# PSUM banks dealt out anew in a gated S4D and Infini-attention kernel: maxima, spreading products, and the last segment's skip

## The chip, the cores and the metric

The kernel runs on one core of one Trainium2 chip. The metric is the device time of one execution in microseconds, lower is better. Before the change three runs took 926.03, 926.98 and 929.62 us; the median is 926.98.

## What is computed

The input is one sequence `x` of 2048 rows and 448 channels. Two branches are computed from it and mixed by a gate `g = sigmoid((x * gate_w).sum(-1))`:

```
a   = fftconv(x, K) + x * D_skip        # K: an S4D kernel of 2048 taps for each channel
q, k, v = x @ wq, x @ wk, x @ wv        # 16 heads of 28, 4 segments of 512 rows
for each segment s:
    a_dot = softmax(q k^T / sqrt(28) + causal mask) v
    a_mem = phi(q) M / (phi(q) z + 1e-6)       # M, z: sums over earlier segments
    o     = sigmoid(beta) a_mem + (1 - sigmoid(beta)) a_dot
    M, z  = M + phi(k)^T v, z + sum phi(k)     # phi(t) = t + 1 if t > 0 else exp(t)
b   = o @ wo
out = g * a + (1 - g) * b
```

For the first segment `M` and `z` are zero.

## The kernel before, in words

**Two halves.** The first half (`first_half`, to about 497 us) makes the S4D kernel's taps and projects q, k and v. The change does not touch it. The second half (`second_half`) does the attention and the convolution, and everything below belongs to it.

**PSUM in the second half.** PSUM has eight banks of 128 x 512 floats. `psum_pool` deals them out by tags, and `k.ps(tag)` takes the next buffer of a tag by turns: "m" one bank, "a" three buffers of two banks, "pv" one bank. TensorE's instructions stay in program order (`k.mm`, `k.tr`). A product into a buffer waits until whoever reads the buffer's last contents has finished. The order of VectorE, ScalarE, GpSimd and SP is laid by a planner that simulates the timeline, except for what is pinned (`k.pin`) or put behind a mark (`k.dma`, `k.ldma`).

**Attention in groups.** There are 16 groups, i = 4 * segment + head group, of four heads (of 32 partitions each). A group passes through three generators.

- `maxima(i)` finds the row maxima of the scores in six steps, each for one pair of heads and one of three pieces of the causal triangle: piece 0 is 512 columns, piece 1 is 384 and 128, piece 2 is 256. A step takes one "a" buffer, a head to each bank. VectorE adds the mask and takes the maximum in one operation (L927, followed by a short read of the accumulator into `mx`). After six steps four transposes (L1270) bring `mx` into "m", ScalarE (L937) and VectorE (L938) negate it into `mn`, and a DMA issued by GpSimd (L939) writes it into the q tile, so that the weights' product subtracts the maximum by itself.
- `weigh(i)` computes the scores again, transposed, in six steps with an "a" buffer each. ScalarE takes the exponential into `PT` (L958), and GpSimd masks the diagonal (L969).
- `values(i)` multiplies `PT` by V into "pv", and ScalarE copies that into `pvs` (L989).

**The loop.** In round i there are six steps; each issues one step of maxima(i + 2), one of weigh(i), and in groups 1 to 12 on average 1.15 steps of the convolution (`RATIO`). In the second step the values of group i - 1 and the last step of maxima(i + 1) come in between. Before the loop, `transform_k` runs eight blocks with two "a" buffers each, and maxima(0) is interleaved with it; then come maxima(1), with the transposes of maxima(0) behind its third step, and in round 0 maxima(2) beside weigh(0).

**The convolution** (`convolve`) is a product in the frequency domain: for each of 32 chunks `transform` (TensorE into "a", ScalarE copy L569 to `ks`), `product` (TensorE into "a", VectorE multiply L574 to `pr`), and for every second one `back` (eight products into "a", ScalarE copy L587, store). In rounds 14 and 15 `finish` does the last transform in eight calls of `last`: eight products into "a", two VectorE operations (L638) that add the gated result to a tile `rest`, and stores. `join` loads `rest` from TB, `load_b` loads the products' input `bt`.

**Between segments** (`seg_end`): `norm` divides the values by the softmax sums. The sums go through DMAs (`dn`, `RD`, `r8`), and one product per head group (L1267, `ps_m<-r,sel`) spreads the four reciprocals over 32 partitions each. VectorE multiplies (L1046) and adds the memory part (L1048). `recall` does the same for the memory of the next segment (VectorE L1024). Between them four products with `wo` (po) are copied by ScalarE (L1062); `skip` loads a tile of x, multiplies it by `D_skip` (`k.dbc`) on GpSimd (L1056), and `store` adds it, gated, on VectorE (L1063). All these products, and the transposes of the maxima, share the one bank "m". The last segment is treated differently: `skip_last` (called in round 11) writes only the gated skip to TB, `norm(3, 0, 3)` normalises three head groups in round 15, and `last_end` does the fourth through a product with `den` and adds the attention part last.

In `skip_last` GpSimd multiplies by `D_skip` (L1056) and VectorE then by the gate (L1071, a tensor_scalar).

Of the kernel before, what the change touches and what calls it, by code (L numbers as in the profile page):

```python
# [12 lines left out]
F32 = mybir.dt.float32  # L13
# [4 lines left out]
ALU = mybir.AluOpType  # L18
# [5 lines left out]
D = 448  # L24
# [3 lines left out]
SEG = 512  # L28
# [843 lines left out]
def attend(nc, k, ap):  # L872

    v = nc.vector
# [30 lines left out]
    PLACES = ([(0, 0, 512)], [(1, 0, 384), (3, 384, 128)], [(2, 0, 256)])  # L905

    def maxima(i):


        q, kk = Q[i], K[i]  # L910
        mx = ap.tile([128, 4, 4], F32, tag="mx", name="mx", bufs=2)
        for b, hp in MSTEPS:
            pt = k.ps("a")
            for t, o, n in PLACES[b]:
                qt = 3 - t
                for x in range(2):
                    h = 2 * hp + x
                    r = slice(32 * h, 32 * h + 32)
                    k.mm(
                        pt[:, x, o : o + n], q[r, 0, 128 * qt : 128 * qt + 128], kk[r, 0, :n],  # L920
                        start=True, stop=True, tile_position=(32 * h, 0),
                    )
            for t, o, n in PLACES[b]:
                for x in range(2):
                    h = 2 * hp + x
                    junk = ap.tile([128, SEG], F32, tag="jk", name="jk", bufs=1)
                    v.tensor_tensor_reduce(  # L927
                        junk[:, :n], pt[:, x, o : o + n], k.mk[:, SEG - n :], 1.0, -3e38,
                        ALU.add, ALU.max, mx[:, 3 - t, h : h + 1],
                    )  # L930
            yield
        yield
        pm = k.ps("m")
        for qt in range(4):
            k.tr(pm[:4, 128 * qt : 128 * qt + 128], mx[:, qt], k.ident)
        mn = ap.tile([4, 2, SEG], F32R, tag="mn", name="mn", bufs=2)
        nc.scalar.activation(mn[:, 0], pm[:4], AF.Copy, scale=-1.0)  # L937
        v.scalar_tensor_tensor(mn[:, 1], pm[:4], -1.0, mn[:, 0], ALU.mult, ALU.subtract)  # L938
        k.pdma(q.rearrange("(j e) i q -> e j i q", e=32)[28].bitcast(F32), mn.bitcast(F32))  # L939
        yield  # L940
# [51 lines left out]
    def inverse(x, rows, h0, h1, dst, queue):  # L992


        f = 16 * (h1 - h0)
        rc = ap.tile([128, 64], F32, tag="rc", name="rc", bufs=1)
        rs = ap.tile([128, 2, 64], F32R, tag="rs", name="rs", bufs=1)
        v.reciprocal(rc[:, :f], x)
        v.tensor_copy(rs[:, 0, :f], rc[:, :f])
        v.tensor_tensor(rs[:, 1, :f], rc[:, :f], rs[:, 0, :f], ALU.subtract)  # L1000
        rd = k.dr.tile([2, 4, 32 * f], F32, tag=f"RD{f}", name="RD", bufs=2)
        queue(rd.rearrange("b j (i f) -> (j i) b f", f=f), rs[:, :, :f].bitcast(F32))
        queue(
            dst[rows : rows + 8, h0:h1].rearrange("p h q -> p (h q)").bitcast(F32),
            rd.rearrange("b j q -> (b j) q"),
        )
# [3 lines left out]
    def recall(s):  # L1010

        am[s] = ap.tile([128, 4, SEG], F32, tag="am", name="am", bufs=1)
        k.ldma(am[s], k.AM[:, :, s - 1].rearrange("h p q -> p h q"))
        dn = ap.tile([128, 64], F32, tag="dm", name="dm", bufs=1)
        k.ldma(dn, k.DM[s - 1].rearrange("j h (i f) -> (j h i) f", f=64))
        k.pin(v.tensor_scalar(dn, dn, 1e-6, None, ALU.add))
        r8[s] = ap.tile([40, 4, SEG], F32R, tag="r8", name="r8", bufs=1)
        inverse(dn, 32, 0, 4, r8[s], k.pdma)
        for _ in range(3):
            yield  # L1020
        for hg in range(4):
            pb = k.ps("m")
            k.mm(pb, k.sel[32:40], r8[s][32:40, hg], start=True, stop=True)
            v.scalar_tensor_tensor(am[s][:, hg], am[s][:, hg], k.gh[:, hg : hg + 1], pb, ALU.mult, ALU.mult)  # L1024
            yield

    def norm(s, h0, h1, queue):

        pvs = pvss[s]
        f = 16 * (h1 - h0)  # L1030
        dn = ap.tile([128, 64], F32, tag="dn", name="dn", bufs=1)
        for j in range(4):
            queue(
                dn[32 * j : 32 * j + 32, :f],
                pvs[32 * j + 28 : 32 * j + 29, h0:h1].rearrange("o h q -> o (h q)").rearrange("o (i f) -> o i f", f=f),
            )
        if s == 0:
            r8[s] = ap.tile([40, 4, SEG], F32R, tag="r8", name="r8", bufs=1)
        inverse(dn[:, :f], 0, h0, h1, r8[s], queue)
        for _ in range(4):  # L1040
            yield
        for hg in range(h0, h1):
            o = pvs[:, hg]
            pb = k.ps("m")
            k.mm(pb, k.sel[0:8], r8[s][0:8, hg], start=True, stop=True)
            v.scalar_tensor_tensor(o, o, k.omg[:, hg : hg + 1], pb, ALU.mult, ALU.mult)  # L1046
            if s > 0:
                v.tensor_tensor(o, o, am[s][:, hg], ALU.add)  # L1048
            yield

    def skip(s, t):

        i = 4 * s + t
        xt = ap.tile([128, D], F32, tag="xt", name="xt", bufs=4)
        k.ldma(xt, k.u[128 * i : 128 * i + 128])
        k.pin(nc.gpsimd.tensor_tensor(xt, xt, k.dbc, ALU.mult))  # L1056
        return xt
# [8 lines left out]
    def skip_last():  # L1066

        for t in range(4):
            xt = skip(3, t)
            i = 12 + t  # L1070
            v.tensor_scalar(xt, xt, k.gt[:, i : i + 1], None, ALU.mult)  # L1071
            k.dma(k.TB[128 * i : 128 * i + 128], xt)

    def out_mm(s, t, po, hgs):
# [6 lines left out]
    def seg_end(s):  # L1081
        yield from norm(s, 0, 4, k.pdma)
        memory = recall(s + 1)
        for t in range(4):
            xt = skip(s, t)
            po = k.ps("m")
            out_mm(s, t, po[:, :D], range(4))
            store(s, t, po[:, :D], xt)
            next(memory)
            yield  # L1090
        yield from memory
# [27 lines left out]

    k.load_wo = load_wo  # L1120
    k.load, k.maxima, k.weigh, k.values, k.seg_end = load, maxima, weigh, values, seg_end
    k.norm, k.last_end, k.skip_last = norm, last_end, skip_last


# [104 lines left out]
def gated_mix(ctx, tc, k):  # L1229
# [72 lines left out]
    def pool(stack, name, side="left"):  # L1302
        return stack.enter_context(tc.tile_pool(name=name, bufs=1, side=side, reuse_waits="tile"))
# [71 lines left out]
    def psum_pool(stack, shapes):  # L1375
        p = stack.enter_context(tc.tile_pool(name="ps", bufs=1, space=PSUM, reuse_waits="tile"))

        def ps(tag):
            shape, bufs = shapes[tag]
            return p.tile(shape, F32, tag=tag, name="ps_" + tag, bufs=bufs)  # L1380

        k.ps = ps
# [44 lines left out]
    with ExitStack() as st:  # L1427
        psum_pool(
            st,
            {"m": ([128, 512], 1), "a": ([128, 2, 512], 3), "pv": ([128, 512], 1)},  # L1430
        )
        ap = pool(st, "ap", "right")
        k.mk = ap.tile([128, 512], F32, name="mk")
        nc.sync.dma_start(k.mk, k.c_mk)
        k.dbc = ap.tile([128, D], F32, name="dbc")
        tp, cs = ExitStack(), ExitStack()

        def fourier():
            tp.close()
            kst.close()  # L1440
            return pool(cs, "fp")

        def final():
            cs.close()
            return pool(st, "fin")

        second_half(nc, k, ap, pool(tp, "tp"), fourier, final)
# [34 lines left out]
```

## Time and profile before

| what | value |
|---|---|
| median of three runs | 926.98 us (926.03 to 929.62) |
| the profiled execution's own time | 931.7 us |
| its span, first to last instruction | 930.0 us |
| mean granted TensorE clock | 0.879 |
| TensorE products, busy | 756.6 us (81%) |
| TensorE weight loads, busy | 410.9 us (44%) |
| VectorE busy | 578.8 us (62%) |
| ScalarE busy | 549.4 us (59%) |
| GpSimd busy | 180.3 us (19%) |
| HBM | 90.92 MB read, 60.68 MB written |

The profile is that of one execution. In its rows PE is TensorE's products, PEld its weight loads, DVE VectorE, ACT ScalarE, POOL GpSimd, and SPq the queue of the engine that issues most DMAs. A row of the timeline gives the start in us from the beginning of the span, the duration of what is merged in it, engine, line, operation, output<-inputs, and the count; in brackets stands the time for which the engine was idle before, and who ended it. A row of a tile or a line gives the shortest, median and longest duration in ns, and the first and last start. A row of the waits gives who waited for whom: the total in us, how often, and the longest. Most products stand under L1267, since one helper issues them; the tile names tell them apart: `ps_a<-ku,qu` are the maxima, `ps_a<-qu,ku` the weights, `ps_a<-gk,cf`, `ps_a<-gu,cf` and `ps_a<-pr,cb` the convolution's three products, `ps_a<-bt,fc` the last transform, `ps_a<-kb,s1k` the first one. The granted clock is 1.0 at full speed.

### The profile page before, as it was taken

The numbers are of one execution on the slowest core, as the hardware profiler recorded it, in microseconds if no ns is written. First come the engines' busy times: TensorE is split into PE (matmuls) and PEld (weight loads), VectorE is DVE, ScalarE is ACT, GpSimd is POOL, SyncE is SP. The second block draws the span as 40 slices with busy tenths as digits, with TensorE's granted clock in tenths as the row PEclk, the third lists the DMA queues.
The fourth block names the chain that finished last, engine by engine and source line by source line (L and its number), as shares of the span: only waits on it lengthen the run. The fifth ranks groups of instructions, "written<-read, shape, count | busy, mean of one in ns | idle before, by whom it ended". The sixth has DMA issues, their size and how long they took to land.

```text
span 930.0 us, 18810 instructions
## 1 busy us (share of the span) xinstructions
PE 756.6 (81%) x7426; PEld 410.9 (44%) x7426; DVE 578.8 (62%) x1122; ACT 549.4 (59%) x659; POOL 180.3 (19%) x228
## 2 busy tenths in 40 slices
PE   2428968998889987899877699889987998978957
PEld 1314635655456544465533254444443443334423
DVE  8981776477665876657754856655574757565333
ACT  4645798788897898978892244544454444332300
POOL 3821001110011011110010021222312223223210
PEclk9858998999789999899987858988999998688968
DMA  8664622353233433234445984574565654564971
GB/s 212 205 207 142 204 79 71 110 166 126 79 129 101 155 116 113 89 100 160 160 140 200 372 261 148 181 236 157 176 209 189 196 198 157 185 219 127 267 210 39
DMA packets 85786, 153.21 MB, mean 165 GB/s; under 512 B 20034, under 2 KB 53818, under 8 KB 85650
## 3 DMA queue, kind: packets, MB, share of 16 engines
q1 hardware_dynamic: 78434, 140.88, 47.3%
q10 hardware_dynamic: 5792, 9.86, 3.0%
q0 software_dynamic: 1472, 1.27, 0.5%
q8 instruction: 58, 0.95, 0.4%
q14 instruction: 30, 0.25, 0.1%
HBM read 90.92 MB, written 60.68 MB: 163 GB/s over the span
## 4 chain that ended last, share of the span: by engine, by line
PE 49%; DVE 13%; ACT 13%; DMA 12%; issue 6%; SPq 4%; POOL 2%; ACTq 0%; DVEq 0%; POOLq 0%
PE ps_m L1267 19%; PE ps_a L1267 15%; PE ps_arg L1267 5%; PE ps_k L1267 4%; ACT cs L1239 4%; PE ps_pv L1267 3%; DVE jk L927 3%; DVE Y L385 2%; PE ps_m L1270 2%; ACT L1239 2%; SPq L322 2%; DMA dn<-pvs 1%; DVE X L381 1%; DMA qu<-mn 1%; DVE pr L574 1%
## 5 line engine op out<-in xcount | busy, mean ns | idle before, releaser
L927 DVE CUSTOM_DVE_ANT_0 jk<-ps_a,mk 128x512 f32<-128x512 f32 (+3 forms) x256 | 124.9, 488 | 45.2 <-PE ps_a L1267 38.3
L958 ACT ACTIVATE PT<-ps_a 128x1024 f32<-128x1024 f32 (+1 forms) x96 | 84.3, 881 | 112.6 <-PE ps_a L1267 107.7
L347 POOL TENSOR_TENSOR EX<-EX,cab 128x1024 f32<-128x1024 f32 x28 | 53.6, 1913 | 367.8 <-ACT EX L1239 367.8
L1239 ACT ACTIVATE cs<-ps_arg 128x1024 f32<-128x1024 f32 x112 | 108.1, 1019 | 7.1 <-PE ps_arg L1267 5.9
L1267 PE MATMUL ps_a<-qu,ku 32*128 32x512 f32 (+3 forms) x768 | 97.3, 380 | 5.4 <-DMA qu<-mn 2.8
L1267 PE MATMUL ps_m<-xh,w 112*128 112x512 f32 x256 | 95.1, 423 | 4.5 <-DMA w<-WD 3.0
L1267 PE MATMUL ps_k<-Y,X 128*32 128x64 f32 x3584 | 68.7, 235 | 25.3 <-DVE Y L386 25.3
L381 DVE TENSOR_TENSOR X<-EX,cs 128x1024 f32<-128x1024 f32 x56 | 68.4, 1221 | 25.3 <-ACT cs L1239 23.0
L1267 PEld LDWEIGHTS ps_k<-Y,X 128*32 128x32 f32 x3584 | 59.1, 119 | 54.3 <-DVE Y L386 40.0
L969 POOL TENSOR_SCALAR_AFFINE_SELECT PT<-PT 128x256 f32<-128x256 f32 (+1 forms) x96 | 47.5, 497 | 177.2 <-ACT PT L958 166.9
L1267 PEld LDWEIGHTS ps_a<-qu,ku 32*128 32x128 f32 x768 | 67.6, 211 | 18.0 <-DVE mx L927 6.7
L387 DVE SCALAR_TENSOR_TENSOR Y<-EY,cs 128x512 f32<-128x512 f32 x56 | 38.5, 687 | 48.1 <-ACT cs L1239 39.9
L385 DVE TENSOR_TENSOR Y<-EY,cs 128x1024 f32<-128x1024 f32 x56 | 68.3, 1219 | 0.0
L1239 ACT ACTIVATE cs<-cs,bhp 128x1024 f32<-128x1024 f32 x56 | 64.4, 1150 | 1.8
L1267 PE MATMUL ps_a<-ku,qu 32*128 32x512 f32 (+3 forms) x256 | 50.5, 425 | 17.8 <-DVE mx L927 16.6
L1267 PEld LDWEIGHTS ps_m<-xh,w 112*128 112x128 f32 x256 | 49.4, 193 | 30.2 <-issue 15.1
L1239 ACT ACTIVATE EY<-ps_arg 128x1024 f32<-128x1024 f32 x55 | 56.2, 1040 | 6.8 <-PE ps_arg L1267 6.7
L1267 PEld LDWEIGHTS ps_a<-ku,qu 32*128 32x128 f32 x256 | 24.2, 203 | 78.5 <-DVE mx L927 41.7
L1267 PE MATMUL ps_m<-xl,w 112*128 112x512 f32 x128 | 51.4, 401 | 0.0
L1267 PE MATMUL ps_arg<-ct,lh 64*128 64x512 bf16 x224 | 43.3, 400 | 8.8 <-ACT cs L1239 8.3
L574 DVE TENSOR_TENSOR pr<-ps_a,ks 128x896 f32<-128x896 f32 x32 | 34.8, 1086 | 20.7 <-PE ps_a L1267 19.8
L1267 PEld LDWEIGHTS <-lh 64*128 64x128 bf16 x392 | 21.8, 97 | 57.7 <-issue 41.9
(193 smaller groups left out, 1375.5 us busy)
## 6 DMA issues: line engine op xcount, KB each, us to landing
w<-WD SPq DMA_DIRECT2D x32, 448.0 KB
qu<-QD SPq DMA_DIRECT2D x16, 512.0 KB
ku<-KD SPq DMA_DIRECT2D x16, 512.0 KB
GU<-gs SPq DMA_DIRECT2D x32, 224.0 KB
GK<-gs SPq DMA_DIRECT2D x8, 896.0 KB
gk<-GK SPq DMA_DIRECT2D x32, 224.0 KB
gu<-GU SPq DMA_DIRECT2D x32, 224.0 KB
BB<-bs ACTq DMA_DIRECT2D x16, 448.0 KB
```

Of the source, the lines that this page charges most:

```text
L322: nc.sync.dma_start(lt[J][r, c], k.SD[0:2, :, pc, :, n].rearrange("f s q j n -> (f s) (q j) n"))
L347: nc.gpsimd.tensor_tensor(o, o, cab, ALU.mult)
L381: v.tensor_tensor(X, ex, t[:, :, 0], ALU.mult)
L385: v.tensor_tensor(Y[:, :, :, :32], lo, y[:, :, :, ::-1], ALU.mult)
L387: v.scalar_tensor_tensor(Y[:, 1, :, 32:], ey[:, :, 32:], -1.0, y[:, 1], ALU.mult, ALU.mult)
L574: nc.vector.tensor_tensor(pr[c], pt, ks.pop(c), ALU.mult)
L927: v.tensor_tensor_reduce(junk[:, :n], pt[:, x, o : o + n], k.mk[:, SEG - n :], 1.0, -3e38, ALU.add, ALU.max, mx[:, 3 - t, h : h + 1],)
L958: nc.scalar.activation(PT[:, 2 * hp : 2 * hp + 2, 512 * b : 512 * b + n], pt[:, :, :n], AF.Exp, scale=SCALE)
L969: nc.gpsimd.affine_select(sl, sl, pat, ALU.is_ge, 0.0, base=0, channel_multiplier=-1)
L1239: x = op(*args, **kw)
L1267: tc.keep_in_program_order(nc.tensor.matmul(*args, **kw))
L1270: tc.keep_in_program_order(nc.tensor.transpose(*args))
```

## The change

The eight banks are dealt out anew: "a" has two buffers of two banks, not three, and the two banks go to a new tag "x" with two buffers of one bank. A step of maxima takes two "x" tiles, one for each of its two heads, where it took one "a" tile. VectorE reduces one head's pieces first and then the other's, where it alternated between heads; the products' order stays. `recall` puts its spreading products into "pv" in place of "m"; `norm` uses "pv" for even head groups and "m" for odd ones. In `skip_last` the GpSimd product and the tensor_scalar become one VectorE operation with two tensor inputs and the gate as a scalar; loads and stores are the same.

```diff
@@ maxima @@
-            pt = k.ps("a")
+            pt = [k.ps("x") for _ in range(2)]
             for t, o, n in PLACES[b]:
                 qt = 3 - t
                 for x in range(2):
                     h = 2 * hp + x
                     r = slice(32 * h, 32 * h + 32)
                     k.mm(
-                        pt[:, x, o : o + n], q[r, 0, 128 * qt : 128 * qt + 128], kk[r, 0, :n],
+                        pt[x][:, o : o + n], q[r, 0, 128 * qt : 128 * qt + 128], kk[r, 0, :n],
                         start=True, stop=True, tile_position=(32 * h, 0),
                     )
-            for t, o, n in PLACES[b]:
-                for x in range(2):
+            for x in range(2):
+                for t, o, n in PLACES[b]:
                     h = 2 * hp + x
                     junk = ap.tile([128, SEG], F32, tag="jk", name="jk", bufs=1)
                     v.tensor_tensor_reduce(
-                        junk[:, :n], pt[:, x, o : o + n], k.mk[:, SEG - n :], 1.0, -3e38,
+                        junk[:, :n], pt[x][:, o : o + n], k.mk[:, SEG - n :], 1.0, -3e38,
                         ALU.add, ALU.max, mx[:, 3 - t, h : h + 1],
                     )
@@ recall @@
-            pb = k.ps("m")
+            pb = k.ps("pv")
@@ norm @@
-            pb = k.ps("m")
+            pb = k.ps(("pv", "m")[hg % 2])
@@ skip_last @@
-            xt = skip(3, t)
             i = 12 + t
-            v.tensor_scalar(xt, xt, k.gt[:, i : i + 1], None, ALU.mult)
+            xt = ap.tile([128, D], F32, tag="xt", name="xt", bufs=4)
+            k.ldma(xt, k.u[128 * i : 128 * i + 128])
+            v.scalar_tensor_tensor(xt, xt, k.gt[:, i : i + 1], k.dbc, ALU.mult, ALU.mult)
             k.dma(k.TB[128 * i : 128 * i + 128], xt)
@@ gated_mix, second half @@
-            {"m": ([128, 512], 1), "a": ([128, 2, 512], 3), "pv": ([128, 512], 1)},
+            {"m": ([128, 512], 1), "a": ([128, 2, 512], 2), "x": ([128, 512], 2), "pv": ([128, 512], 1)},
```

## The prediction, written before the result was known

> **What bounds the kernel now.** The page's first line gives the span; then I read the windows view, the waits, the timeline.
>
> ```profile
> span 930.0 us, 18810 instructions
> ```
>
> All edits lie behind 497 us, where the first product over ps_a starts. Two stretches of the windows view (at the end of a row stand the granted clock, the DMA engines' busy share and GB/s):
>
> ```profile
> 497.00:546.00 49.00, 38.55 (x235) 20.26 (x235) 33.76 (x108) 15.49 (x18) 3.82 (x8) 0.74 0.96 327
> 546.00:862.00 316.00, 277.86 (x1838) 127.31 (x1842) 185.35 (x530) 135.21 (x166) 79.34 (x134) 0.88 0.56 185
> ```
>
> In the long middle TensorE is busy 277.9 of 316.0 us, VectorE 185.4, ScalarE 135.2: TensorE sets the pace, and only its 38 idle us and its clock (0.88) can give anything. The waits of TensorE from 540 to 860 us say who ends that idle time:
>
> ```profile
> PE ps_a L1267 <- DVE mx L927: 13.4, 18, 3.4
> PE ps_a L1267 <- DVE pr L574: 10.2, 15, 4.4
> PE ps_m L1267 <- ACT tb L1062: 3.6, 5, 0.7
> PE ps_m L1267 <- DVE am L1024: 2.9, 4, 1.0
> ```
>
> The columns are us in total, times, the longest. The first row is the maxima; the 4.4 in the second is the last segment's skip, as shown below; the last two are users of the single bank "m" that wait for each other.
>
> **Part 1, the maxima's own banks: +3.2 and -0.5 us.** In the steady loop (groups 1 to 12) a step allocates one tile for maxima, one for weights, one or two for the convolution. With three buffers by turns, and three tiles a step, each kind reuses its own last tile. With two of "a" for weights and convolution and "x" for maxima that stays so. So no distance in the loop changes, but for the steps with two convolution products, where the second now waits for the weights' exponentials of its step; held against the starts of the trace, one place is short:
>
> ```profile
> 777.41 1.02 ACT L958 ACTIVATE PT<-ps_a 128x1024 f32<-128x1024 f32 x1 [0.50 <-PE ps_m L1267]
> ```
>
> ```profile
> 778.14 1.02 PE L1267 MATMUL ps_a<-gu,cf 64*128 64x448 f32 x4
> ```
>
> The buffer comes free at 778.43, the product began at 778.14: **+0.3**.
>
> What does the split of heads buy? TensorE runs in order, and a step's second head still waits for the last reduction of the step before: the first may start sooner, but the weights behind the second may not. VectorE saves the 0.48 us for which it waits on TensorE after such a stall:
>
> ```profile
> 562.30 0.42 DVE L927 CUSTOM_DVE_ANT_0 jk<-ps_a,mk 128x256 f32<-128x256 f32 x1 [0.48 <-PE ps_a L1267]
> ...
> 563.56 1.09 DVE L574 TENSOR_TENSOR pr<-ps_a,ks 128x896 f32<-128x896 f32 x1 [0.35 <-ACT PT L958]
> ```
>
> Here the next product idles 0.35 us anyway, so the 0.48 is not worth anything. The ends are 0 and the 13.4 us of the first wait row; I take **-0.5**, nearest to this row.
>
> Before the loop it costs. Where nothing but maxima runs, three buffers let TensorE go three steps ahead of the reductions; two banks of one head each let it go one. Group 1's third step and, queued right behind it on TensorE, group 0's four transposes (L1270) stand here:
>
> ```profile
> 524.04 0.50 PE L1267 MATMUL ps_a<-ku,qu 32*128 32x384 f32 x4 [0.37 <-DVE mx L927]
> 524.47 0.60 PE L1270 MATMUL ps_m<-ident,mx 128*4 128x128 f32 x4
> ...
> 534.21 0.79 PE L1267 MATMUL ps_a<-qu,ku 32*128 32x512 f32 x2 [1.90 <-DMA qu<-mn]
> ```
>
> ```profile
> 527.06 0.08 DVE L927 DVE_READ_ACCUMULATOR2_ANT mx<- 128x1 f32 x1
> 527.06 0.67 DVE L938 SCALAR_TENSOR_TENSOR mn<-ps_m,mn 4x512 fp32r<-4x512 f32 x1
> ```
>
> ```profile
> L939 POOL DMA_DIRECT2D qu<-mn x16: 560/595/755, 528.4 to 864.7; - x16
> ...
> DMA to landing us min/median/max: 2.1/3.5/6.9
> ```
>
> Afterwards that third step's second head waits for the second step's reductions, which end at 527.14, not 524.0. The transposes then start near 527.9 (the four products before them take 0.5 and more, with the clock at 0.74 in this stretch), take 0.6 to 1.0, the ScalarE negation about as long as this VectorE operation, 0.67, and that operation itself stands behind a reduction under way: the DMA leaves near 531.0 in place of 528.4, 2.6 later. The first weights at 534.21 wait for that DMA (1.90 us), and the loop's work is queued behind them. To it comes the start: the second block of the first transform begins on the third tile at 500.89 us, and with two it waits for the first copy, to 502.06.
>
> ```profile
> 500.89 0.34 PEld L1267 LDWEIGHTS ps_a<-kb,s1k 32*128 32x128 f32 x2 [0.41 <-issue]
> 501.14 0.92 ACT L530 ACTIVATE gs<-ps_a 128x896 f32<-128x896 f32 x1 [3.46 <-PE ps_a L1267]
> ```
>
> That is 1.2 us; I count half of it, since the DMA engines are busy for 0.96 of the stretch and may be what is late there: 2.6 + 0.6 = **+3.2**. The lower end is 0 (the DMA lands in 2.1 us rather than the 5.8 from 528.4 to 534.2), the upper 4.9 (6.9 us, and the full 1.2).
>
> From 864 us the last transform's products lose a buffer too: each waits for VectorE's two operations on the one before.
>
> ```profile
> L638 DVE SCALAR_TENSOR_TENSOR rest<-ps_a,gt,rest x16: 674/680/685, 865.8 to 896.2; 128x448 f32<-128x448 f32 x16
> ```
>
> ```profile
> 874.06 1.12 SPq L1283 DMA_DIRECT2D rest<-TB  x2
> ...
> 887.30 3.26 PE L1267 MATMUL ps_a<-bt,fc 128*64 128x448 f32 x8 [6.10 <-DMA bt<-BB]
> ```
>
> Five products that can be put off lie ahead of the one at 887.30, by at most 2 x 0.68 us each: 6.8 at the very most. Behind each stand group 14's or 15's weights on TensorE, and on SP the stores of its result. The cover is the 6.10 us for which TensorE waits for a load; SP issues that load behind the rest loads at 874.06, which wait for earlier stores to free their buffers. I take 0, and 0.7 as the upper end; with that cover gone it would be up to 6.8.
>
> **Part 2, spreading products: -2.8 and +0.6.** They leave bank "m" for "pv" (every second one of the first kind). These waits go:
>
> ```profile
> 672.43 0.49 PE L1267 MATMUL ps_m<-r,sel 8*128 8x512 f32 x1 [0.72 <-ACT tb L1062]
> 823.90 0.54 PE L1267 MATMUL ps_m<-r,sel 8*128 8x512 f32 x1 [0.84 <-DVE pvs L1046]
> 830.68 0.50 PE L1267 MATMUL ps_m<-r,sel 8*128 8x512 f32 x1 [1.39 <-DVE mn L938]
> ```
>
> The first stands ahead of the recall of segment 2; the same 0.7 stands ahead of that of segment 3 (two of the five waits of the "tb" row above). Of the last two (2.23) I count the 1.4 that VectorE's chain behind them lets through: 2.8 together. The ends are 0 and 4.2, which adds a third "tb" wait and the whole 2.23 and leaves nothing to VectorE. Late next is that chain, two operations for each head group. Successive products of the recall share "pv" as they shared "m", so their 2.9 us of waits stay. A new wait stands at the end: the last group's value product needs "pv" while the third spreading product's bank is still read.
>
> ```profile
> 904.14 4.50 PE L1267 MATMUL ps_pv<-PT,V 128*32 128x512 f32 x32
> 904.32 0.75 DVE L1046 SCALAR_TENSOR_TENSOR pvs<-pvs,omg,ps_m 128x512 f32<-128x512 f32 x1 [0.23 <-PE ps_m L1267]
> ```
>
> That operation ends at 905.07, some 0.3 sooner with the second product on "m": 904.75 against 904.14, **+0.6**. Behind it queue the sum over "den" and the last outputs. Lower end 0, upper 0.9.
>
> **Part 3, the skip: -3.0, and -3.0 by the clock.** Four GpSimd products (4.39 us) lock VectorE out:
>
> ```profile
> 785.31 4.39 POOL L1056 TENSOR_TENSOR xt<-xt,dbc 128x448 f32<-128x448 f32 x4
> ```
>
> ```profile
> 786.50 4.32 DVE L1071 TENSOR_SCALAR xt<-xt,gt 128x448 f32<-128x448 f32 x2 [0.16 <-POOL xt L1056]
> ```
>
> ```profile
> 791.87 3.25 PE L1267 MATMUL ps_a<-pr,cb 128*64 128x448 f32 x8 [4.39 <-DVE pr L574]
> ```
>
> ```profile
> L1071 DVE TENSOR_SCALAR xt<-xt,gt x4: 438/515/3814, 786.5 to 792.6; 128x448 f32<-128x448 f32 x4
> L1063 DVE SCALAR_TENSOR_TENSOR tb<-xt,gt,tb x12: 684/804/2627, 652.2 to 851.9; 128x448 f32<-128x448 f32 x12
> ```
>
> One of the four took 3.81 us beside GpSimd, the median 0.5. The new operation is of L1063's kind and size: 0.69 undisturbed. Loads and stores on SP are the same, GpSimd's queue loses 4.4 us. VectorE was free at 786.34 (786.50 less 0.16). If two stand ahead of "pr" there, as now, "pr" is held up by 2 x 0.69 = 1.4 us, and TensorE waits 1.4 us, not 4.39: **-3.0**. With all four ahead it is -1.6, with none -4.4.
>
> The Trainium skill ("SBUF - State Buffer", Who interferes with whom) says that a VectorE instruction with two SBUF inputs contends with a GpSimd instruction reading SBUF. L1063's 2.63 agrees: the new form is exposed as well, and this speaks against the change (fourth rival).
>
> After the stall TensorE runs at half rate:
>
> ```profile
> 787.50:791.90 4.40, 0.03 (x2) 0.03 (x2) 4.40 (x4) 1.02 (x1) 3.07 (x5) 0.79 0.17 61
> 791.90:807.30 15.40, 15.25 (x60) 6.06 (x64) 7.74 (x25) 4.97 (x6) 1.68 (x3) 0.51 0.62 200
> ```
>
> At the full rate those 15.25 us would be 7.8 (x 0.51); VectorE's 7.74 and the 1.4 of skip left for it make it 9.1: 6.3 to gain if the low stretch comes from the stall alone, 0 if not. I take about half, **-3.0**.
>
> **Sum:** 3.2 + 0.3 - 0.5 - 2.8 + 0.6 - 3.0 - 3.0 = -5.2 us. The profiled execution took 931.7 us (span 930.0, 1.7 around it), so 926.5 by it; it is 4.7 above the median of 926.98, for which I say **921.8**. Chance 0.38, own range 918 to 925.
>
> **Rivals.** (1) *The stretch at half rate stays* (chance 0.24): the 1.4 us left idle, or anything else, still triggers it. For it: such a stretch stands at 619 us with no stall of that size before it.
>
> ```profile
> 619.40:636.50 17.10, 15.94 (x73) 6.35 (x77) 8.05 (x25) 5.08 (x6) 3.32 (x7) 0.50 0.43 144
> ```
>
> Then the sum is -2.2: 924.8. (2) *The split unlocks the loop* (0.10): TensorE's 13.4 us behind the maxima halve because VectorE gets ahead. Against it: the 0.48 row. 6 more: 915.6. (3) *Slower: the lost lead at the start decides* (0.15). If that VectorE operation stands behind another step's reductions (1.8 us) and its DMA takes the longest time, part 1 costs 3.2 + 1.8 + 1.1 = 6.1; with the skip at -1.6, no clock gain, half of the 2.8 and the small terms (+0.4): +3.5, 930.5. For it: VectorE has no idle time there into which the operation would fit. Against the small gains it decides from 2.6 us on (first weights at 536.8), against the forecast's (8.4) from 542.6. (4) *The skip's stall doesn't go* (0.08): the four new operations are held by GpSimd's masks or their loads for as long as now; only the other parts are left, 3.2 + 0.3 - 0.5 - 2.8 + 0.6: +0.8, 927.8. (5) *The stall lowers the clock only briefly* (0.05): for as long again as its own 4.4 us, and the rest of the stretch belongs to the work in it: 2.2 in place of 3.0, 922.6. Against it: no row shows the clock come back within those 15.4 us. The Trainium skill ("TensorE: Matmul & The Clock Gate", What's actually happening) lets one busy window of about 3.4 us bring the full clock back. The 15.25 busy us at 0.51 do not agree with it.
>
> **Range and chances.** From the forecast, no cost of part 1 (3.2), the whole clock gain (3.3) and the skip without a wait (1.4) reach 914; rival 3 gives 930.5. Range **914 to 931**. A measurement here can tell about 0.5% (4.6 us): faster means below 922.3. About two thirds of the forecast's chance, rival 2 and some of rivals 1 and 5 lie there: **0.42**; slower, most of rival 3 and what I overlooked in VectorE's order, which the planner lays anew: **0.14**; the same **0.44**.
>
> **What would show it.** The first maxima's DMA near 531 instead of 528.4 and the first weights near 537 instead of 534.2 (part 1); no ps_m product ended by "tb" on the recall, and the last value product ended by VectorE (part 2); four operations of 0.69 us, no TensorE idle over 2 us near 788, and the clock of the 15 us behind it (part 3). It would be wrong if the planner moved VectorE's reciprocals, which wait for DMAs, to other places, or if new idle time brought half-rate stretches elsewhere.

## The result and the profile after

The changed kernel took 933.16 us (median of 17 runs, 929.61 to 947.86), the kernel before 929.62 in the same session: ratio **1.0054, 95% interval 1.0027 to 1.0080**. It is slower by half a per cent, where 5 us faster had been forecast. Two repeats gave 0.9997 (0.9957 to 1.0037), which is no difference, and 1.0038 (1.0014 to 1.0063); all 41 runs of it average 933.3 us, 139 of the kernel before 930.1. Single runs scatter by 4 to 5 us around their mean. The ratios leave out runs over 1.5% above a kernel's fastest (in e4_early below that is seven of 12), so the mean of all runs is told too.

The page of the changed kernel, and two stretches of its windows view (columns as before: busy us of PE, PEld, DVE, ACT, POOL, then the granted clock):

```profile
span 939.3 us, 18894 instructions
```

```profile
497.00:546.00 49.00, 39.76 (x217) 20.46 (x217) 30.75 (x95) 12.91 (x15) 2.57 (x5) 0.74 0.96 332
546.00:862.00 316.00, 291.74 (x1813) 133.32 (x1811) 181.18 (x532) 133.72 (x164) 74.63 (x128) 0.84 0.53 177
```

In the same 316 us TensorE is busy 13.9 us more than before and does less (1813 products, before 1838): its idle time fell from 38 to 24 us, but the clock fell from 0.88 to 0.84. This execution (941.45 us) is 8 us above the median, so part of that is scatter. What scatters less is the order of events. The start, as forecast (transposes, first DMA of the maxima, first weights):

```profile
527.87 1.01 PE L1271 MATMUL ps_m<-ident,mx 128*4 128x128 f32 x4
537.73 1.68 PE L1268 MATMUL ps_a<-qu,ku 32*128 32x512 f32 x12 [2.04 <-DMA qu<-mn]
```

```profile
531.03 0.76 POOL L939 DMA_DIRECT2D qu<-mn  x1 [57.89 <-DVE mn L938]
```

The forecast had 527.9, "near 531" and "near 537". In two more traces of the changed kernel the first weights start at 531.26 and 537.15, since the second half as a whole begins sooner there; that one trace met the figures is in part luck. The skip: VectorE's four operations (the last three in one row) and, in a second view, the product of TensorE that stands behind them:

```profile
793.91 0.69 DVE L1072 SCALAR_TENSOR_TENSOR xt<-xt,gt,dbc 128x448 f32<-128x448 f32 x1 [0.53 <-DMA xt<-in_A_u]
796.28 1.88 DVE L1072 SCALAR_TENSOR_TENSOR xt<-xt,gt,dbc 128x448 f32<-128x448 f32 x3 [1.68 <-DMA xt<-in_A_u]
```

```profile
799.61 0.44 PE L1268 MATMUL ps_x<-ku,qu 32*128 32x384 f32 x1 [2.17 <-DVE mx L927]
```

GpSimd no longer holds anything up, but VectorE, idle for 0.53 and 1.68 us, now waits for the loads of u themselves, and the maxima's reductions stand behind it. The last part of what I looked for is the maxima's products. One row for all 256 of them (from 500 to 930 us; busy us and mean ns, then the idle time before them and who ended it), first before, then after:

```profile
L1267 PE MATMUL ps_a<-ku,qu 32*128 32x512 f32 (+3 forms) x256 | 50.5, 425 | 17.8 <-DVE mx L927 16.6 <-DVE pr L574 0.5 <-DVE gs L532 0.4
```

```profile
L1268 PE MATMUL ps_x<-ku,qu 32*128 32x512 f32 (+3 forms) x256 | 70.3, 450 | 16.2 <-DVE mx L927 15.6
```

The same products, with nearly the same mean of one, keep TensorE busy for 20 us more. The two heads' products used to run side by side: the second started within 0.1 us of the first in 94 of 96 steps. Now it does so in 58; in the other 38 its own bank is still being reduced when the first starts.

**The theories.** A: the lead lost at the start is the cost, and the rest comes to nothing. B: the split by heads costs in every step, by one more wait on VectorE (96 more in the trace; 84 instructions more in all). C: chance decides, by where TensorE's half-rate stretches fall. After the first four runs two were added. D1: products one behind the other instead of side by side. D2: depth. A step of the maxima had one of three shared buffers, and could go ahead of the reductions by up to three; now it has nothing but the banks that the step before must leave.

### The profile page after: what moved, and what is told of

It reads as the page before. It is cut to its first block, busy times and chain, and to the rows that moved or that the text cites. A ratio compares the mean times of both kernels' runs of the same rounds, so it can differ in the third digit from the quotient of the medians.

```text
span 939.3 us, 18894 instructions
## 1 busy us (share of the span) xinstructions
PE 774.4 (82%) x7425; PEld 419.9 (45%) x7426; DVE 576.6 (61%) x1122; ACT 549.2 (58%) x659; POOL 176.6 (19%) x224
## 4 chain that ended last, share of the span: by engine, by line
PE 50%; DMA 14%; ACT 12%; DVE 12%; issue 5%; SPq 3%; POOL 3%; ACTq 0%; DVEq 0%; POOLq 0%
PE ps_m L1268 17%; PE ps_a L1268 14%; PE ps_arg L1268 5%; PE ps_k L1268 4%; PE ps_pv L1268 4%; ACT cs L1240 4%; DVE jk L927 3%; PE ps_x L1268 3%; DVE Y L385 2%; PE ps_m L1271 2%; SPq L322 2%; ACT L1240 2%; DVE X L381 1%; SPq L1284 1%; DVE pr L574 1%
## 5 line engine op out<-in xcount | busy, mean ns | idle before, releaser
L927 DVE CUSTOM_DVE_ANT_0 jk<-ps_x,mk 128x512 f32<-128x512 f32 (+3 forms) x256 | 124.8, 487 | 58.7 <-PE ps_x L1268 42.5
L1268 PE MATMUL ps_a<-qu,ku 32*128 32x512 f32 (+3 forms) x768 | 99.6, 389 | 3.4 <-DMA qu<-mn 2.0
L1268 PE MATMUL ps_x<-ku,qu 32*128 32x512 f32 (+3 forms) x256 | 70.3, 450 | 16.2 <-DVE mx L927 15.6
L1268 PEld LDWEIGHTS ps_x<-ku,qu 32*128 32x128 f32 x256 | 33.4, 210 | 88.7 <-DVE mx L927 48.6
L1268 PE MATMUL ps_pv<-PT,V 128*32 128x128 f32 (+3 forms) x512 | 52.5, 566 | 1.8 <-DVE pvs L1046 1.8
L1268 PE MATMUL ps_m<-xl,w 112*128 112x512 f32 x128 | 51.4, 401 | 0.0
```

What stands on the lines that cost most here:

```text
L927: v.tensor_tensor_reduce(junk[:, :n], pt[x][:, o : o + n], k.mk[:, SEG - n :], 1.0, -3e38, ALU.add, ALU.max, mx[:, 3 - t, h : h + 1],)
L1268: tc.keep_in_program_order(nc.tensor.matmul(*args, **kw))
```

## The experiments

All of them were timed in five rounds, 12 runs each (6 in the run with two buffers). "Diff." is the mean of all runs less the mean of the kernel before in the same session.

| run | diff. us | ratio (95%) |
|---|---|---|
| e1_banks: part 1 alone | +7.4 | 1.0085 (1.0052 to 1.0119) |
| e2_spread: part 2 alone | -2.7 | 0.9982 (0.9946 to 1.0017) |
| e3_skip: part 3 alone | -3.8 | 0.9985 (0.9948 to 1.0023) |
| e4_early: changed kernel, transposes earlier | +3.9 | 0.9990 (0.9942 to 1.0039) |
| e5_pair: changed kernel, heads in the other order | +2.1 | 1.0032 (0.9995 to 1.0069) |
| e6_onebuf: changed kernel, two banks as one buffer | +1.5 | 1.0025 (0.9990 to 1.0061) |
| e7_two_three: parts 2 and 3 | -9.5 | 0.9911 (0.9879 to 0.9942) |
| e8_after_again: changed kernel | +1.1 | 0.9997 (0.9957 to 1.0037) |
| e9_start_shared: groups 0 and 1 on shared buffers | +10.1 | 1.0070 (1.0037 to 1.0103) |
| e10_early_loads: parts 2 and 3, loads issued earlier | -6.8 | 0.9948 (0.9915 to 0.9981) |
| e11_two_three_again: parts 2 and 3 | -6.3 | 0.9937 (0.9903 to 0.9971) |
| e12_one_group: group 1 on shared buffers | -1.2 | 0.9999 (0.9974 to 1.0023) |
| e13_two_buffers: parts 2 and 3, ring of two | +127.4 | 1.1377 (1.1327 to 1.1426) |
| e14_after_third: changed kernel | +2.6 | 1.0038 (1.0014 to 1.0063) |

**The three parts by themselves.** Each is its hunk of the diff above, on the kernel before.

> Only the maxima's two banks of their own; spreading products and skip as before. Theory A (the lead lost at the start, 3.1 us, is what costs; the loop itself gains or loses nothing by the split): 3 to 4 us above the kernel before, so 1.003 to 1.004, and all of it there by the first weights (near 537.7 instead of 534.2). Theory B (each step of the maxima has one more wait on VectorE, the second head's bank, 0.11 us by 96 steps, and the planes are taken by fewer buffers): 6 to 9 us above, 1.006 to 1.010, growing through the rounds. Theory C (what differs is where the half-rate stretches of TensorE fall): anything between 0.997 and 1.010, with no tie to the shift at the first weights.

> Only the products that spread reciprocals moved (recall's to the values' bank, norm's to that and the small bank by turns). Theories A and B, as the prediction has it: 2 us below the kernel before, 0.997 to 0.999; the waits of ps_m for pvs are gone and last value product waits 0.6 to 1.8 us for VectorE. Theory C: between 0.995 and 1.003.

> Only the last segment's skip in one VectorE operation. As predicted (the stall near 790 falls from 4.39 to 1.4 us and the half-rate stretch behind it halves): 4 to 6 us below the kernel before, 0.993 to 0.996. The rival (VectorE's operations now wait for the loads of u themselves, the stall falls only to some 2.8 us and the half-rate stretch stays, as in the trace of after): 1 to 2 us below, 0.998 to 0.999. Theory C: 0.996 to 1.003, the half-rate stretch is there at full length wherever the stall ends.

Part 1 alone costs 7.4 us (2.8 either way), more than theory A's 3 to 4. Parts 2 and 3 gain 2.7 and 3.8 (forecast: 2.2 and 6.0), too little each to be told from no change by itself. In e3 the stall beside the skip is 2.90 us, not 4.39; in e2, without part 3, it is still 4.40.

**The lead, given back by moving the transposes.**

```diff
+    step(ms[0])
+    step(ms[0])
-    for r in range(3):
-        step(ms[1])
-    step(ms[0])
-    step(ms[0])
-    for r in range(3):
+    for r in range(6):
         step(ms[1])
```

> The changed kernel with the last two steps of group 0's maxima (its four transposes and the transfer of the maxima) moved ahead of the first three steps of group 1's. Theory A: the first maxima's transfer is issued near 525 to 528 and the first weights are back near 532 to 534; 3 to 4 us below the changed kernel, so 1.000 to 1.002 of the kernel before. Theory B: the start is won back but the loss in the rounds stays; TensorE waits for VectorE at the transposes instead; 0 to 2 us below the changed kernel, 1.003 to 1.006. Theory C: a shift at the start is given back by other half-rate stretches; 1.002 to 1.006.

The DMA does leave early, 528.29, but the first weights come no earlier (two views of this run):

```profile
528.29 0.76 POOL L939 DMA_DIRECT2D qu<-mn  x1 [56.74 <-DVE mx L927]
```

```profile
537.87 1.64 PE L1266 MATMUL ps_a<-qu,ku 32*128 32x512 f32 x6
```

No idle time is noted on them: the products of the maxima that stand ahead on TensorE are late themselves. The mean of all 12 runs is 3.9 us above the kernel before, as the changed kernel's is (933.3 against 930.1). So the DMA isn't what holds the start, and theory A's account of it falls.

**The split, taken back in two ways.** In e5 the matmul loop runs over `x in (1, 0)`. In e6 the pool alone is divided:

```diff
-            pt = [k.ps("x") for _ in range(2)]
+            pt = k.ps("x")
...
-"x": ([128, 512], 2)
+"x": ([128, 2, 512], 1)
```

with products into `pt[:, x, ...]` and reductions in the order of the kernel before.

> The changed kernel with the two heads' products issued in the other order, so that the bank that comes free last is waited for first. In the trace of the changed kernel the second head's product starts more than 0.1 us behind the first in 38 of 96 steps (it waits for its own bank), in the kernel before in 2, and the maxima's products keep TensorE busy 70.3 instead of 50.5 us. Theory D1 (one product behind the other instead of side by side is what the change lost): the pairs start together again, 50 to 54 us busy, and 4 to 6 us below the changed kernel. Theory D2 (it is only waiting that is now counted as work; the loss is that a step of the maxima has no buffer but the one that the step before it leaves, instead of one of three): the pairs start together, 50 to 54 us busy, TensorE's idle time before them grows by as much, and the time stays within 2 us of the changed kernel, or up to 2 us above it.

> The changed kernel with the maxima's two banks as one buffer, products and reductions as before: the pool alone is divided, not the heads. Theory D2 (the depth lost: the maxima's steps have one buffer instead of three shared ones): as slow as the changed kernel or up to 3 us slower, 1.003 to 1.009 of the kernel before; the stretch from the second maxima step to the first weights of group 1 stays at 43 to 45 us (40.4 before). Theory B or D1 (it is the split by heads, by its 96 more waits on VectorE, 0.11 us each, or by its products one behind the other): 4 to 6 us below the changed kernel, 0.999 to 1.002, and that stretch at 40.5 to 42 us.

e5 didn't do what it was made for: in its trace the heads are still more than 0.1 us apart in 38 of 96 steps. e6 did: 95 of 96 pairs start together, and VectorE's extra waits are gone (18800 instructions). Its row of the maxima's products:

```profile
L1268 PE MATMUL ps_x<-ku,qu 32*128 32x512 f32 (+3 forms) x256 | 51.6, 438 | 33.2 <-DVE mx L927 33.1
```

Busy time is back at 51.6, and the idle time before the products has gone up to 33.2. The time is that of the changed kernel (+1.5, against +1.1 for the changed kernel on the same chip). **Theories B and D1 fall**: most of the 20 us of more "busy" were waiting under another name.

**Parts 2 and 3 without part 1, and the changed kernel on the same chip.** The hunks of `maxima` and of the pool are left out.

> The kernel before with the second and third part alone: spreading products in two banks, the skip in one operation, the maxima in the three shared buffers as before. If the parts add up as in the two runs by themselves (2.7 and 3.8 us below the mean of before): 4 to 7 us below the kernel before, 0.993 to 0.996. If their gains were scatter of the clock: 0.997 to 1.001.

> The changed kernel unchanged, on the same chip as the others and for a second trace. Every theory expects 1.003 to 1.008 of the kernel before, the stretch from the second maxima step to group 1's first weights at 43 to 44 us again, and (theory C) half-rate stretches of TensorE at other places than in the first trace, the stall beside the skip at 2.5 to 3 us again.

> Second and third part on the kernel before, again, as the measure for the other two on the same chip and to see whether 0.991 holds: 0.988 to 0.995 of the kernel before. If the first run of it was scatter: above 0.995.

0.9911 and 0.9937: **this version beats both kernels**, by 6 to 9 us the one before. Its 24 runs average 922.1 us, the changed kernel's 41 933.3: on top of the other parts, part 1 costs 11.2 (2.2 either way), so chance alone (theory C) doesn't make it. e8 lies below what every theory expected, e7 a little below its range. The same row in the second run of it, against e6's:

```profile
L1268 PE MATMUL ps_a<-ku,qu 32*128 32x512 f32 (+3 forms) x256 | 51.4, 432 | 20.2 <-DVE mx L927 19.4 <-DVE gs L532 0.4
```

Busy 51.4 against 51.6, idle 20.2 against 33.2: 13 us more waiting before the same products when the only difference is whose buffer they may take. On one chip, e6 stands 11 us above e7 (+1.5 against -9.5).

**Depth.** e9 gives four of six maxima steps of groups 0 and 1 a shared buffer (`i < 2` in the first diff), e12 those of group 1 alone; e13 is e11 with a ring of two (second diff).

```diff
-        for b, hp in MSTEPS:
-            pt = [k.ps("x") for _ in range(2)]
+        for n_, (b, hp) in enumerate(MSTEPS):
+            if i == 1 and n_ % 3 < 2:
+                both = k.ps("a")
+                pt = [both[:, 0], both[:, 1]]
+            else:
+                pt = [k.ps("x") for _ in range(2)]
```

```diff
-            {"m": ([128, 512], 1), "a": ([128, 2, 512], 3), "pv": ([128, 512], 1)},
+            {"m": ([128, 512], 1), "a": ([128, 2, 512], 2), "pv": ([128, 512], 1)},
```

> The changed kernel, but four of the six maxima steps of groups 0 and 1 take the shared buffers (two of three in order, the third their own banks), so that before the loop a step waits for the reductions of the step three before it, as in the kernel before. In the four traces with shared buffers the stretch from the second maxima step to group 1's first weights takes 39.4 to 40.4 us, in the six with banks of their own 43.4 to 45.8. Theory D2 (the lost depth is the cost, most of it at the start): that stretch back at 39.5 to 41 us, and the time 4 to 6 us below the changed kernel, 0.995 to 0.999 of the kernel before. If the start is only a part of it and the loop loses too (half-rate stretches, 132 us behind 497 us with shared buffers, 145 with own): 0.998 to 1.002, and half-rate time still above 138 us. If the depth isn't it: the stretch stays at 43 us or more, 1.002 to 1.006.

> As the run with groups 0 and 1 on shared buffers, but for group 1 alone, whose six maxima steps follow one another with no other product that needs a shared buffer between them; group 0's stay in their own banks, so that the transform's products keep both shared ones. Theory D2 (depth): the stretch from the second maxima step to group 1's first weights falls from 43.4 to 40 to 42 us, and the time 1.5 to 4 us below the changed kernel's. If the start isn't what costs: the stretch may fall, the time stays within 1 us of the changed kernel's.

> Second and third part, with the shared ring cut to two buffers of two banks and no bank for the maxima alone (two banks stay unused). Theory D2 (what counts is how many buffers a step can go ahead of the reductions and evictions): slower than the changed kernel (which has two shared and one own), 1.006 to 1.025 of the kernel before, with more idle time of TensorE than in any other run. If depth doesn't matter: 0.990 to 0.996, as second and third part with three buffers.

> The changed kernel unchanged, a third time, as the measure for the other two on the same chip: 1.001 to 1.006 of the kernel before by every theory; the half-rate time behind 497 us between 140 and 157 us as in its two traces so far.

e13 goes off by 14%, where 0.6 to 2.5% had been expected: in the windows view TensorE is busy 267 of 316 us at a clock of 0.68.

```profile
546.00:862.00 316.00, 267.23 (x1325) 122.55 (x1326) 134.18 (x408) 101.14 (x122) 50.09 (x91) 0.68 0.44 141
```

So one buffer in three is worth 135 us here (1057.6 against 922.1), and the two banks of their own give most of that back, but not the last 11.

The expected texts take a stretch "from the second maxima step to group 1's first weights"; their figures start at group 0's first step (for e9 the figure of 41.86 starts at its third). From the first step (the difference of the starts) it is 40.79 us in e12, in the changed kernel's trace beside it 43.83, with three shared buffers 39.38 to 40.68. e12's time is 3.7 us below the changed kernel's on the same chip (-1.2 against +2.6). Its first weights and those of e14, where the first maxima step had begun 1.8 us sooner:

```profile
534.67 1.64 PE L1272 MATMUL ps_a<-qu,ku 32*128 32x512 f32 x6
```

```profile
537.15 1.68 PE L1268 MATMUL ps_a<-qu,ku 32*128 32x512 f32 x12 [2.09 <-DMA qu<-mn]
```

**Theory D2 holds at the start**, and e9 shows both sides of it. Between group 1's first maxima step and the first weights lie 14.5 us in the changed kernel's traces, 11.6 to 12.0 with three shared buffers, 11.5 in e12 and 11.6 in e9. But in e9 group 0's steps took buffers that the first transform's products need; these waited 2.5 us for VectorE's copies (0.6 in e11), and group 0's six steps are spread over 23.9 us, in the changed kernel's traces over 14.3 to 14.6, with three shared buffers over 14.9. The whole stretch from the first maxima step to group 1's first weights is 50.20 us:

```profile
500.96 0.50 PE L1272 MATMUL ps_a<-ku,qu 32*128 32x512 f32 x2 [0.60 <-ACT gs L530]
...
551.16 1.65 PE L1272 MATMUL ps_a<-qu,ku 32*128 32x512 f32 x6
```

That is 6 to 7 us more than in the changed kernel, and its runs average 10.1 us above the kernel before, 6.8 more than the changed kernel's. Its profiled run, 928.31 us, is the fastest of the 12 and has their highest granted clock, 0.892 (mean 0.875): luck, not a gain.

**The first transform.** These stretches leave out a cost that lies ahead of the first maxima step. A block of the first transform takes two shared buffers at once; when there are only two, each block waits for the copies of the one before. e14, then e11, from the first product of the second half to the first maxima step:

```profile
493.52 3.37 PE L1268 MATMUL ps_a<-kb,s1k 32*128 32x448 f32 x16 [1.77 <-ACT gs L1240]
497.89 3.59 PE L1268 MATMUL ps_a<-kb,s1k 32*128 32x448 f32 x16 [1.00 <-ACT gs L530]
502.27 3.77 PE L1268 MATMUL ps_a<-kb,s1k 32*128 32x448 f32 x16 [0.78 <-ACT gs L530]
505.15 1.29 PE L1268 MATMUL ps_x<-ku,qu 32*128 32x512 f32 x2
```

```profile
496.46 6.98 PE L1268 MATMUL ps_a<-kb,s1k 32*128 32x448 f32 x36 [1.76 <-ACT gs L1240]
503.71 1.77 PE L1268 MATMUL ps_a<-kb,s1k 32*128 32x448 f32 x12 [0.27 <-ACT gs L530]
504.97 0.74 PE L1268 MATMUL ps_a<-ku,qu 32*128 32x512 f32 x2
```

The first product of the second half is the last event that all kernels share. Counted from it, the traces of the three runs with parts 2 and 3 and three shared buffers (e7, e10, e11) and of the six with own banks for all maxima (the changed kernel, e4, e5, e6, e8, e14) don't overlap:

| us from the second half's first product | three shared | own banks | changed kernel's three |
|---|---|---|---|
| to the first maxima step | 7.4 to 8.5 | 8.8 to 11.6 | 8.8, 8.8, 11.6 |
| to group 1's first weights | 46.8 to 49.2 | 52.2 to 57.4 | 52.2, 52.3, 55.5 |
| to the end | 421.5 to 427.8 | 434.9 to 442.0 | 442.0, 435.5, 434.9 |

By the means of three traces each, 53.3 against 48.3, **the start is about 5 of the 11 us**. What lies behind group 1's first weights overlaps: 372.5 to 378.6 us against 377.7 to 389.7.

**The loads of the skip.** `skip_last` was cut in two, the four loads at r = 0 of round 11 and the operations at r = 2, on top of parts 2 and 3.

> Second and third part on the kernel before, with the four loads of u for the skip issued two steps of the loop earlier than the VectorE operations that read them. In the run without this VectorE waits 2.2 us for the loads and TensorE then 2.53 us for the maxima. If the loads are what is left of the stall: no wait of VectorE for them, TensorE's stall at 1.5 us or less, 0.5 to 2 us below the kernel with second and third part. If it is the four operations themselves (2.7 us): the stall stays at 2.3 us or more, same time. If the loads now hold up others on SP's queue: 1 to 3 us above.

The edit didn't move the loads: SP issued them 4.6 us ahead of the first operation (771.80, 776.42), without it 4.3 (777.87, 782.15), and VectorE waits 2.5 us for them, TensorE 2.81. So the run tells nothing of earlier loads; that was not tried in another way.

## Why the prediction was wrong

**The step that failed** is the price of part 1, +3.0 us: +3.2 for the start and +0.3 - 0.5 for the loop, where "no distance in the loop changes". It measured +7.4 alone and 11.2 on top of the other parts, while those came out near their forecast. Two terms were too small. The start costs about 5 us; the 0.6 in it for the first transform, half of 1.2, measures 1.6 (8.8, 8.8 and 11.6 us against a mean of 8.1 with the shared ring; 11.6 in e4, e5 and e6, too). And some 6 us lie behind group 1's first weights, where the prediction had next to nothing.

One place in the loop shows a distance that did change. "No distance changes" holds where a step of the loop allocates three tiles. Where it has two, for maxima and weights alone, the ring of three lets the next maxima step take a buffer that is free already. Such are the six steps of round 0, two of round 12, where the convolution runs out, and the six of round 13. Parts 2 and 3 with the ring of three (e11), from the convolution's product at 806.31 on, in round 12:

```profile
806.31 1.72 PE L1268 MATMUL ps_a<-pr,cb 128*64 128x448 f32 x8
807.96 0.44 PE L1268 MATMUL ps_a<-ku,qu 32*128 32x384 f32 x2
...
809.05 0.50 PE L1268 MATMUL ps_a<-ku,qu 32*128 32x384 f32 x4
810.39 1.08 PE L1268 MATMUL ps_a<-qu,ku 32*128 32x384 f32 x12 [0.84 <-DVE mx L927]
...
813.16 0.58 PE L1268 MATMUL ps_a<-ku,qu 32*128 32x256 f32 x2 [0.74 <-DVE mx L927]
...
814.30 0.58 PE L1268 MATMUL ps_a<-ku,qu 32*128 32x256 f32 x2
```

and the same steps where the maxima have one buffer of their own (e6):

```profile
813.52 1.72 PE L1268 MATMUL ps_a<-pr,cb 128*64 128x448 f32 x8
815.17 0.45 PE L1268 MATMUL ps_x<-ku,qu 32*128 32x384 f32 x2
...
817.61 0.44 PE L1268 MATMUL ps_x<-ku,qu 32*128 32x384 f32 x2 [1.33 <-DVE mx L927]
...
821.46 0.58 PE L1268 MATMUL ps_x<-ku,qu 32*128 32x256 f32 x2 [1.81 <-DVE mx L927]
...
823.26 0.58 PE L1268 MATMUL ps_x<-ku,qu 32*128 32x256 f32 x2 [0.79 <-DVE mx L927]
```

From the convolution's product to the last maxima step shown it takes 7.99 us with three shared buffers and 9.74 with one of its own. The second maxima step starts 1.09 us behind the first in the one and 2.44 in the other, because it waits for the first one's reductions. With the shared ring that wait falls on the weights behind it, 0.84 us, when VectorE is already at work on the second step. The prediction compared the distances by counting tiles in an average step; not all steps of the program are like it.

But this place doesn't account for the 6 us. From the first of these maxima steps to group 15's first one it takes 11.3 and 11.6 us in e11 and e7, 12.2 in e6, and 11.4 to 11.8 in the changed kernel's three traces. Round 13 takes 31.6 to 32.7 us with the shared ring (e7, e10, e11) and 32.0 to 34.6 in the changed kernel.

**The clock** has a part in it. The granted clock of whole runs averages 0.876 in the changed kernel (41 runs) and 0.885 in parts 2 and 3 (24 runs). Among runs of one and the same kernel a clock higher by 0.01 goes with a time some 4.7 us shorter, so 0.009 goes with about 4 of the 11 us. That is no term beside the others: half-rate time lies in the start (22 to 29 us up to group 1's first weights with the shared ring, 28 to 40 with own banks) as well as behind it, and whether the waits bring the lower clock was not shown. So the division of the ring is the cause (e6 against e7, where nothing else differs), about 5 us of its cost are traced to the start, and **what the other 6 consist of stays open**.

The other points, in the prediction's order:

- *Start, +3.2*: too small, as said, and its cause half wrong. It hangs on the first DMA of the maxima; e4 sends that at 528.29 and wins nothing, since six maxima steps in a row are paced by their own reductions. e12, which gives these a shared ring again, wins 3.7 back.
- *Last transform, 0*: right, and for the reason given. The products that lost a buffer now wait, and TensorE's wait for the load that covers them shrinks from 6.10 to 2.5 us (first row below).
- *Part 2, -2.2*: -2.7 measured, which fits, but is no more than the scatter. Only two of the five waits for "tb" are left; at the end the last value product waits 1.8 us, where the prediction had 0.6. Waits of TensorE from 862 us on, changed kernel:

```profile
PE ps_a L1268 <- DMA bt<-BB: 2.5, 1, 2.5
PE ps_pv L1268 <- DVE pvs L1046: 2.2, 2, 1.8
```

- *Part 3, -3.0 and -3.0*: -3.8 measured. With the shared ring (e3, e7, e10, e11) the stall fell to 2.5 to 2.9 us instead of 1.4, because all four operations and the wait for their loads stand ahead of the reductions: the fourth rival's mechanism, in part. The half-rate stretch behind it did not shorten; in the changed kernel it is this one, longer than before:

```profile
800.90:821.40 20.50, 20.35 (x95) 8.48 (x95) 8.85 (x27) 7.02 (x8) 2.50 (x5) 0.50 0.31 110
```

- *Parts 2 and 3 together, -8.2*: right, -9.5 and -6.3, though not by the clock gain that the prediction had put behind the skip.
- *Rival 3* (slower, 930.5, chance 0.15) had the sign and nearly the number, in part by luck. Its 6.1 us for part 1, all at the start, is near what the traces show there, though it put them on a late DMA. But it had nothing for the loop, and only 2.6 us of gain elsewhere, where parts 2 and 3 brought 6 to 9: the two errors cancel.

## What to carry to other kernels

Before a shared ring of buffers is divided by use, count for every place that uses it, the one ahead of the loop too, and not for an average step, how far each user could go ahead before and after; where a step has fewer tiles than the ring has buffers, dividing takes depth away. Count time from the last event that both kernels share: what scatters ahead of it then drops out. Read busy and idle time of a group together: products that wait in the middle of their group for a bank count as busy. Measure the parts of a change one by one: here two of three were worth 0.6 to 0.9%, and the third ate them.

## What the runs showed of the hardware

- Two products of 32 rows each, on different row groups, run side by side when both may start: 256 of a mean of 425 ns (108.8 us in sum) kept TensorE busy for 50.5 us.
- Half rate lasts long while TensorE is busy: 20.35 of 20.50 us at a clock of 0.50 (row above) and, in the kernel before, 15.25 of 15.40 at 0.51. The Trainium skill ("TensorE: Matmul & The Clock Gate", What's actually happening) has the full clock come back after one busy window of about 3.4 us; these rows don't agree.
- Unchanged code scatters too: the first product of the second half began between 490.9 and 499.9 us in these traces, though all share the code ahead of it. One trace against one trace says little below 5 us; the order of events and the waits say more.
